# First block's steps in another order: G's two parts in unused accumulator banks, E's coefficients as a spare row of G2

## The chip, the cores and the metric

The kernel runs on one core of one Trainium2 chip. The metric is device time in microseconds; the time before is the median of five runs. A core's engines work side by side, each on a queue of its own in program order: TensorE (PE, its weight loads PEld), VectorE (DVE), ScalarE (ACT), GpSimd (POOL), and SyncE (SP), which issues most DMA transfers. An instruction that waits holds up everything behind it on its engine.

## The reference

Two layers, in float32. The first mixes each of 8 sequences with a two-dimensional Fourier transform and keeps the real part; the second is a two-layer network with a squared ReLU over all 24064 rows.

```python
# x: (8, 3008, 256)   w_in: (256, 2048)   w_out: (2048, 256)
X = np.fft.fft(np.fft.fft(x, axis=1), axis=2).real
h = X.reshape(24064, 256) @ w_in
r = np.maximum(h, 0.0)
out = (r * r) @ w_out
```

## The kernel before

The transform along the sequence becomes, for each sequence b, three arrays in SBUF: Pt (cosine part, 128 rows), Qt (sine part, 127 rows) and Et (one column of the transform, repeated on 128 partitions), each over 1505 positions. VectorE folds the input rows by symmetry (lines L356 to L386), TensorE multiplies the folded rows with cosine and sine tables (`even_n` and `odd_n`, L455 and L500, into a PSUM tile pd), and VectorE joins the partial sums (L468 to L472, tiles db, dc, then Pt, Qt, Et).

The transform along the 256 features is put into the weights instead. For each pair of 128-column chunks j of w_in (j = 0 to 7), `products` multiplies the chunk with a cosine table (cosd) and a sine table (sind, 127 columns) on TensorE into a tile pg, and ScalarE copies the two results into G1 and G2 (L263). The coefficient gE of Et is a third product, of the chunk with a column of alternating signs (altd): eight matmuls of one column (L268), halved by ScalarE into gE (L270).

The weights arrive as 64-bit floats. `convert` loads one chunk with two DMAs on SP's queue (tile raw, one of four buffers, three of which also serve the input tiles) and makes float32 of it. Its opening is two VectorE instructions (L234, L239) and three on ScalarE (L236, L237, L241); the function `finish` that it returns issues three more on VectorE (L244, L246, L247). There are 16 conversions: `load_win(j)` for w_in, tiles win, and `load_wout(j)` for w_out, tiles wout. Intermediate tile fd has two buffers, m three.

The second layer runs in steps (b, block of 251 positions, j). A step i has:
- `front`: for each of two halves h, TensorE makes hP and hQ from G1 with Pt and G2 with Qt (L551, L552), in one of two PSUM banks tagged h; VectorE adds gE times Et (L554, tile he) and forms the sum and the mirrored difference (L556, L557, tile g).
- `combine`: ScalarE applies ReLU and square (L566, L567) to g; after the first block GpSimd also forms four sums (L574 to L577).
- `back`, two steps later (LAG = 2): TensorE accumulates the product with wout in banks mA to mD. The first block uses a plain form with mA and mB alone (L591); later blocks use a form with seven products (L604).
- `gather` and `store` after the eighth j.

PSUM's eight banks are: two tagged h, two tagged d, and mA, mB, mC, mD, one each. Before the change G's products take banks of tag h, the tag of the fronts, and E's product a bank of tag d.

The order of the first eight steps is written out by hand. The conversions stand in a list, win0, win1, wout0, win2, wout1, win3 and so on, and `next_weight` opens the next one, then finishes the one opened before it, and returns its products. Ahead of the loop win0, win1 and wout0 are finished and win2 is opened. Each step of the first block then issues front, combine, back, the products of one win, and up to two calls of `next_weight`:

```python
        for f in products:
            f()
        products = [next_weight() for _ in range(2 if 0 < i < NJ - 2 else 1 if i < NJ else 0)]
```

From step 8 on, `sum_wout` (L282 to L285) and pieces of the next sequence's folding and transform are put between the fronts on VectorE (`between`); the inputs of sequence 1 are requested at step 8 (L158), followed by many small transfers of single columns (L329).

Of the kernel before, what the change touches and what calls it, by code (L numbers as in the profile page):

```python
# [13 lines left out]
P = 128  # L14
# [67 lines left out]
def kernel(  # L82
# [75 lines left out]
        nc.sync.dma_start(out=xt[b, t][0:rows], in_=x[b, r0:r0 + step * (rows - 1) + 1:step])  # L158

    cosd = const.tile([P, 2, P], F32, name="cosd")  # L160
    sind = const.tile([P, 2, P - 1], F32, name="sind")
    altd = const.tile([P, 2, 1], F32, name="altd")
    cosT = const.tile([P, 2, WT], F32, name="cosT")
    sinT = const.tile([P, 2, WT], F32, name="sinT")
    wout = const.tile([P, NJ, 2, 2, H], F32, name="wout")
    wsum = const.tile([P, 3, NJ, H], F32, name="wsum")
    ident = const.tile([P, P], F32, name="ident")
    G1 = const.tile([P, F], F32, name="G1")
    G2 = const.tile([P - 1, F], F32, name="G2")
    gE = const.tile([P, NFC], F32, name="gE")  # L170

    def load_table(tab, src, engine):
# [13 lines left out]
    ramp = const.tile([P, 2], F32, name="ramp")  # L186
    nc.vector.memset(ramp[:, 0:1], 1151.0)
    nc.vector.memset(ramp[:, 1:2], 255.0 * 2.0 ** 23)
    for dst, src in ((cosd, cos_d), (sind, sin_d), (altd, alt_d)):
        nc.scalar.dma_start(out=dst, in_=src.rearrange("(c p) m -> p c m", p=P))  # L190


# [60 lines left out]
    def load_win(j):  # L253

        w = ep.tile([P, 2, CH], F32, name="win", tag="sB" if j % 2 else "sA")
        finish = convert(parts(w, 1), pair_in(j))

        def products():
            for tab, G, n in ((cosd, G1, P), (sind, G2, P - 1)):
                ps = psh.tile([P, CH], F32, name="pg", tag="h")  # L260
                for i in range(2):
                    nc.tensor.matmul(ps[0:n], tab[:, i], w[:, i], start=i == 0, stop=i == 1)
                nc.scalar.copy(G.rearrange("p (h j f) -> j p h f", h=2, j=NJ)[j],  # L263
                               ps[0:n].rearrange("p (h f) -> p h f", h=2))
            ps = psd.tile([P, CH], F32, name="pe", tag="d")
            for h in range(2):
                for i in range(2):
                    nc.tensor.matmul(ps[:, h:h + 1], w[:, i, h * P:(h + 1) * P], altd[:, i],  # L268
                                     start=i == 0, stop=i == 1)
            nc.scalar.mul(gE[:, j::NJ], ps[:, 0:2], 0.5)  # L270

        return finish, products

    def load_wout(j):

        return convert(wout[:, j].rearrange("p h c e -> p h (c e)"), pair_out(j)), lambda: None

    def sum_wout(j):

# [261 lines left out]
    def front(b, k0, n, j, between):  # L541

        pt, qt, et = PQE[b]
        ks = slice(k0, k0 + n)
        g = gp.tile([P, 2, 2, CK], F32, name="g", tag="g")
        for h in range(2):
            fc = j + NJ * h
            fs = slice(fc * P, (fc + 1) * P)
            ps = psh.tile([P, 2, CH], F32, name="ph", tag="h")
            hP, hQ = ps[:, 0, 0:n], ps[:, 1, 0:n]  # L550
            nc.tensor.matmul(hP, G1[:, fs], pt[:, ks], start=True, stop=True)  # L551
            nc.tensor.matmul(hQ, G2[:, fs], qt[:, ks], start=True, stop=True)  # L552
            t = hp.tile([P, CK], F32, name="he", tag="he")[:, 0:n]
            nc.vector.scalar_tensor_tensor(out=t, in0=et[:, ks], scalar=gE[:, fc:fc + 1], in1=hP,  # L554
                                           op0=ALU.mult, op1=ALU.add)
            tt(out=g[:, h, 0, 0:n], in0=t, in1=hQ, op=ALU.add)  # L556
            tt(out=g[:, h, 1, 0:n][:, ::-1], in0=t, in1=hQ, op=ALU.subtract)  # L557
            between()
        return g
# [22 lines left out]
    def back(n, j, g, s, final):  # L582

        if j == 0:
            for nm in ("mA", "mB", "mC", "mD"):
                acc[nm] = psm.tile([P, 2, CH], F32, name=nm, tag=nm)
        if s is None:
            for c in range(2):
                for h in range(2):
                    for side, nm in enumerate(("mA", "mB")):  # L590
                        nc.tensor.matmul(acc[nm][:, h, 0:n], wout[:, j, h, c], g[:, c, side, 0:n],  # L591
                                         start=j == c == h == 0, stop=j == NJ - 1 and c == 1, skip_group_check=True)
            return
        products = [("mA", 0, wout[:, j, 0, 0], g[:, 0, 0]),
                    ("mA", 1, wout[:, j, 0, 1], g[:, 1, 0]),
                    ("mB", 0, wsum[:, 2, j], g[:, 1, 1]),
                    ("mB", 1, wout[:, j, 1, 0], s[:, 0]),
                    ("mC", 0, wsum[:, 0, j], s[:, 1]),
                    ("mC", 1, wsum[:, 1, j], s[:, 2]),
                    ("mD", 0, wout[:, j, 1, 1], s[:, 3])]  # L600
        if final and j == NJ - 1:
            products = products[0:2] + products[4:7] + products[2:4]
        for nm, i, w, v in products:
            nc.tensor.matmul(acc[nm][:, i, 0:n], w, v[:, 0:n], start=j == 0 and i == 0, stop=j == NJ - 1,  # L604
                             skip_group_check=True)

    def gather(n, plain, final):


        mA, mB, mC, mD = (acc[nm] for nm in ("mA", "mB", "mC", "mD"))  # L610
        if plain:
            c = ep.tile([P, 2, 2, CK], F32, name="c", tag="c")
            for side, m in enumerate((mA, mB)):
                nc.scalar.copy(c[:, side, :, 0:n], m[:, :, 0:n])
            return c
        sA = ep.tile([P, 2, CK], F32, name="sA", tag="sA")
        sB = ep.tile([P, 2, CK], F32, name="sB", tag="sB")
        u = ep.tile([P, 3, CK], F32, name="u", tag="u")
        c = ep.tile([P, 2, 2, CK], F32, name="c", tag="c")
        nc.scalar.copy(sA[:, :, 0:n], mA[:, :, 0:n])  # L620
        if not final:
            nc.scalar.copy(sB[:, :, 0:n], mB[:, :, 0:n])
        m1, m2, m4, m5 = sA[:, 0, 0:n], sA[:, 1, 0:n], sB[:, 0, 0:n], sB[:, 1, 0:n]
        u2, u3, u4 = (u[:, i, 0:n] for i in range(3))
        tt(out=u2, in0=m1, in1=mC[:, 0, 0:n], op=ALU.add)
        tt(out=u3, in0=u2, in1=mC[:, 1, 0:n], op=ALU.add)
        tt(out=u4, in0=u2, in1=mD[:, 0, 0:n], op=ALU.add)
        gt = nc.gpsimd.tensor_tensor
        gt(out=c[:, 0, 0, 0:n], in0=m1, in1=m2, op=ALU.add)
        if final:  # L630
            tt(out=c[:, 0, 1, 0:n], in0=u4, in1=mB[:, 1, 0:n], op=ALU.add)
            tt(out=c[:, 1, 1, 0:n], in0=u3, in1=mB[:, 1, 0:n], op=ALU.add)
            tt(out=c[:, 1, 0, 0:n], in0=u3, in1=mB[:, 0, 0:n], op=ALU.subtract)
            return c
        gt(out=c[:, 1, 0, 0:n], in0=u3, in1=m4, op=ALU.subtract)
        gt(out=c[:, 1, 1, 0:n], in0=u3, in1=m5, op=ALU.add)
        gt(out=c[:, 0, 1, 0:n], in0=u4, in1=m5, op=ALU.add)
        return c
# [41 lines left out]
                + groups + [(0.0, lambda: load_e(1))])  # L680


    weights = [lambda j=j: load_win(j) for j in range(2)]
    for j in range(NJ):
        weights.append(lambda j=j: load_wout(j))
        if j + 2 < NJ:
            weights.append(lambda j=j: load_win(j + 2))

    def next_weight():

        nonlocal begun
        (finish, products), begun = begun, weights.pop(0)() if weights else None
        finish()
        return products

    pieces = [fold(0, t) for t in range(NT)]
    start, *groups = [f for _, f in dft_ops(0)]

# [8 lines left out]
    def groups_at(*which):  # L707
        for i in which:
            groups[i]()

    begun = weights.pop(0)()
    for t in range(NT):
        load_x(0, t)
    load_table(cosT, cos_s, nc.sync)
    load_table(sinT, sin_s, nc.sync)
    start()
    for_p(0)
    finish, products = begun
    finish()
    products()  # L720
    for t in range(1, 4):
# [3 lines left out]
    for_q(0)  # L725
    for_q(1)
    groups_at(1, 2)
    for_p(5)
    groups_at(6, 7)
    for_p(6)  # L730
# [4 lines left out]
    groups_at(9, 10)  # L735
    for_q(6)
    groups_at(11, 12, 13)
    begun = weights.pop(0)()
    groups_at(15)
    for_q(2)  # L740
    groups_at(14, 16, 17, 18)
    for_q(3)
    groups_at(20, 19, 25)
    products = [next_weight()]
    groups_at(21, 22, 23, 26, 27, 28)
    next_weight()
    groups_at(24, 29)
    LAG = 2
    BLOCKS = [(k0, min(CK, NKT - k0)) for k0 in range(0, NKT, CK)]
    steps = [(b, k0, n, j) for b in range(B) for k0, n in BLOCKS for j in range(NJ)]  # L750
# [3 lines left out]
    def between():  # L754


        nonlocal spent
        if i < NJ or i % NJ == LAG - 1:
            return
        spent -= pace / 2 if i < 2 * NJ else pace  # L760
        while side and spent <= 0:
            t, f = side.pop(0)
            f()
            spent += t

    flight, finished = [], []
    for i in range(len(steps) + LAG + 4):
        if i < len(steps):
# [12 lines left out]
                spent, pace = 0.0, sum(t for t, _ in side) / (calls - (0 if i else 3 * (NJ - 1)))  # L781
            g = front(b, k0, n, j, between)
            if i < NJ:
                s = combine(n, g, True)
            elif i < 2 * NJ:
                sum_wout(j)
        while finished and finished[0][0] <= i:
            store(*finished.pop(0)[1:])
        if i >= LAG and flight:
# [3 lines left out]
            if at[3] == NJ - 1:  # L793
                c_ = gather(at[2], s_ is None, final)
                finished += [(i + 2 + s, *at[:3], s, c_, final) for s in range(2)]
        for f in products:
            f()
        products = [next_weight() for _ in range(2 if 0 < i < NJ - 2 else 1 if i < NJ else 0)]
        if i < len(steps):
            flight.append(((b, k0, n, j), g, s if i < NJ else combine(n, g, False)))  # L800

# [62 lines left out]
```

## Time and profile before

| What | Value |
|---|---|
| Time, median of 5 runs (range) | 1962.86 us (1962.1 to 1964.76) |
| The profiled execution: time, span | 1963.19 us, 1961.4 us |
| Mean granted TensorE clock | 0.996 |
| Busy in the span: PE, DVE, ACT, POOL | 1924.5, 1399.3, 924.9, 1170.3 us |
| First he (L554) of steps 0, 1, 2, 3 | 53.59, 59.69, 68.19, 76.69 us |
| First he of steps 6, 7, 8, 9, 10 | 102.19, 108.28, 113.32, 118.43, 123.53 us |

Times inside a trace count from the span's first instruction. The profiled execution's own time is 1.8 us longer than its span. A line of a timeline gives start, duration, engine, source line, operation and tiles; what stands in brackets is the idle time just before and who ended it. Instructions of one engine overlap at their ends, so the room that one takes is read from start to start.

### The profile page before, as it was taken

What the parts mean: (1) busy time and instruction counts of PE and PEld (TensorE: products, weight loads), DVE (VectorE), ACT (ScalarE), POOL (GpSimd) and SP (SyncE); (2) the same over time, 40 slices, a digit from 0 to 9 for tenths busy, and PEclk for the clock granted to TensorE, in tenths of its full rate; (3) what the DMA queues carried; (4) which work ended last, traced back from release to release, by engine and by line L of the source; (5) the groups of instructions that cost most, each with busy time, mean ns of one, the idle gap of its engine ahead of it and who ended that gap; (6) DMA issues with size and microseconds to landing.
All of it is one profiled execution on the core that took longest, in us unless ns stands there. A gap on an engine that the chain in (4) does not pass through costs nothing.

```text
span 1961.4 us, 27513 instructions
## 1 busy us (share of the span) xinstructions
PE 1924.5 (98%) x9160; PEld 1705.1 (87%) x9160; DVE 1399.3 (71%) x3434; ACT 924.9 (47%) x1076; POOL 1170.3 (60%) x1705
## 2 busy tenths in 40 slices
PE   5999999999999999999999999999999999999998
PEld 3788888888988899888998889888898888988887
DVE  7888867777677776777668776677767777655554
ACT  1754544455444444444444454444544454444443
POOL 0036745667466755666556765666756676556564
PEclk8999999999999999999999999999999999999999
DMA  7332101211021111111011200121002101100101
GB/s 194 111 45 53 26 13 40 49 27 23 13 51 41 23 26 27 41 33 35 12 35 36 46 20 12 37 52 27 20 16 52 33 11 22 27 11 11 22 11 22
DMA packets 145340, 68.88 MB, mean 35 GB/s; under 512 B 129003, under 2 KB 136110, under 8 KB 145197
## 3 DMA queue, kind: packets, MB, share of 16 engines
q1 hardware_dynamic: 144121, 66.60, 15.6%
q8 instruction: 72, 1.18, 0.3%
q14 instruction: 71, 0.58, 0.1%
q10 hardware_dynamic: 1076, 0.52, 0.1%
HBM read 42.39 MB, written 24.68 MB: 34 GB/s over the span
## 4 chain that ended last, share of the span: by engine, by line
PE 92%; DVE 4%; ACT 1%; DMA 1%; issue 0%; POOL 0%; SPq 0%; DVEq 0%; POOLq 0%; ACTq 0%
PE ph L552 16%; PE ph L551 16%; PE mC L604 16%; PE mA L604 16%; PE mB L604 16%; PE mD L604 8%; PE pd L455 2%; PE pd L500 2%; DVE he L554 1%; DVE g L557 1%; DVE g L556 1%; DMA cosT<-in_cos_s_dram 0%; ACT g L566 0%; ACT g L567 0%; DVE w L386 0%
## 5 line engine op out<-in xcount | busy, mean ns | idle before, releaser
L566 ACT ACTIVATE g<-g 128x1004 f32<-128x1004 f32 (+1 forms) x384 | 399.5, 1040 | 817.7 <-DVE g L557 383.0
L574 POOL TENSOR_TENSOR s<-g 128x251 f32<-128x251 f32 (+1 forms) x376 | 246.0, 654 | 716.2 <-ACT g L567 654.5
L554 DVE SCALAR_TENSOR_TENSOR he<-Et,gE,ph 128x251 f32<-128x251 f32 (+1 forms) x768 | 361.6, 471 | 422.0 <-PE ph L552 421.0
L551 PE MATMUL ph<-Pt,G 128*128 128x251 f32 (+1 forms) x1536 | 451.8, 375 | 4.6 <-ACT G L263 3.4
L552 PE MATMUL ph<-Qt,G 127*128 127x251 f32 (+1 forms) x1536 | 451.4, 374 | 0.4 <-DVE Qt L468 0.4
L567 ACT ACTIVATE g<-g 128x1004 f32<-128x1004 f32 (+1 forms) x384 | 399.3, 1040 | 12.2
L604 PE MATMUL mC<-s,wsum 128*128 128x251 f32 (+1 forms) x1504 | 381.4, 374 | 0.0
L604 PE MATMUL mA<-g,wout 128*128 128x251 f32 (+1 forms) x1504 | 379.8, 374 | 0.0
L556 DVE TENSOR_TENSOR g<-he,ph 128x251 f32<-128x251 f32 (+1 forms) x768 | 320.4, 417 | 54.4 <-POOL s L574 0.5
L551 PEld LDWEIGHTS ph<-Pt,G 128*128 128x128 f32 x1536 | 287.3, 189 | 42.7 <-ACT G L263 4.0
L552 PEld LDWEIGHTS ph<-Qt,G 127*128 127x128 f32 x1536 | 291.2, 190 | 36.6 <-DVE Qt L468 0.8
L604 PEld LDWEIGHTS mC<-s,wsum 128*128 128x128 f32 x1504 | 285.6, 190 | 34.6
L557 DVE TENSOR_TENSOR g<-he,ph 128x251 f32<-128x251 f32 (+1 forms) x768 | 314.1, 409 | 0.0
L604 PEld LDWEIGHTS mA<-g,wout 128*128 128x128 f32 x1504 | 282.8, 189 | 34.8 <-issue 0.6
L575 POOL TENSOR_TENSOR s<-s,g 128x251 f32<-128x251 f32 (+1 forms) x376 | 283.4, 754 | 29.4
L576 POOL TENSOR_TENSOR s<-g 128x251 f32<-128x251 f32 (+1 forms) x376 | 295.4, 786 | 0.0
L577 POOL TENSOR_TENSOR s<-g,s 128x251 f32<-128x251 f32 (+1 forms) x376 | 255.4, 679 | 0.0
L604 PE MATMUL mB<-g,wsum 128*128 128x251 f32 (+1 forms) x752 | 220.5, 374 | 0.0
L604 PE MATMUL mD<-s,wout 128*128 128x251 f32 (+1 forms) x752 | 220.4, 374 | 0.0
L604 PE MATMUL mB<-s,wout 128*128 128x251 f32 (+1 forms) x752 | 219.9, 374 | 0.0
L604 PEld LDWEIGHTS mB<-g,wsum 128*128 128x128 f32 x752 | 142.6, 190 | 17.4
L604 PEld LDWEIGHTS mD<-s,wout 128*128 128x128 f32 x752 | 141.9, 189 | 17.7
(118 smaller groups left out, 1284.0 us busy)
## 6 DMA issues: line engine op xcount, KB each, us to landing
out_dram<-os SPq DMA_DIRECT2D x376, 56.0 KB
xt<-in_x_dram SPq DMA_DIRECT2D x32, 384.0 KB
xt<-in_x_dram SPq DMA_DIRECT2D x42, 128.0 KB
Et<-e_dram SPq DMA_DIRECT2D x7, 752.5 KB
xt<-in_x_dram SPq DMA_DIRECT2D x9, 512.0 KB
out_dram<-os SPq DMA_DIRECT2D x288, 6.8 KB
raw<-in_moe_w_in_dram SPq DMA_DIRECT2D x16, 256.0 KB
raw<-in_moe_w_out_dram SPq DMA_DIRECT2D x16, 256.0 KB
```

The lines of the kernel that those rows point to most:

```text
L551: nc.tensor.matmul(hP, G1[:, fs], pt[:, ks], start=True, stop=True)
L552: nc.tensor.matmul(hQ, G2[:, fs], qt[:, ks], start=True, stop=True)
L554: nc.vector.scalar_tensor_tensor(out=t, in0=et[:, ks], scalar=gE[:, fc:fc + 1], in1=hP, op0=ALU.mult, op1=ALU.add)
L556: tt(out=g[:, h, 0, 0:n], in0=t, in1=hQ, op=ALU.add)
L557: tt(out=g[:, h, 1, 0:n][:, ::-1], in0=t, in1=hQ, op=ALU.subtract)
L566: act(v, v, AF.Relu)
L567: act(v, v, AF.Square)
L574: gt(out=s1, in0=g21, in1=g22, op=ALU.add)
L575: gt(out=s2, in0=s1, in1=g11, op=ALU.subtract)
L576: gt(out=s3, in0=g11, in1=g21, op=ALU.subtract)
L577: gt(out=s4, in0=g12, in1=s2, op=ALU.subtract)
L604: nc.tensor.matmul(acc[nm][:, i, 0:n], w, v[:, 0:n], start=j == 0 and i == 0, stop=j == NJ - 1, skip_group_check=True)
```

## The change

1. The first block's steps get another order. Each step issues front, then (in `weights`) the opening of a wout, the products of win i+1, the finish of win i+2 and the opening of win i+3; then combine and back; then (in `rest`) E's product, the finish of the wout and gE's scaling. wout0 is no longer converted ahead of the loop; wout5 and wout6 are both opened and finished in step 6, wout7 in step 7.
2. G's two products go to the banks mC and mD, which the plain `back` no longer allocates.
3. The alternating column becomes the 128th column of sind, so that G2 has 128 rows, the last of which holds E's coefficients. `for_e` brings that row onto partitions with two products against the last column of the identity (in place of four against altd), and VectorE, in place of ScalarE, halves it into gE. The fronts read the first 127 rows of G2. For win0, `for_e` and its scaling are issued after `groups_at(1, 2)` instead of right after the products.

```diff
-    sind = const.tile([P, 2, P - 1], F32, name="sind")
-    altd = const.tile([P, 2, 1], F32, name="altd")
+    sind = const.tile([P, 2, P], F32, name="sind")
...
-    G2 = const.tile([P - 1, F], F32, name="G2")
+    G2 = const.tile([P, F], F32, name="G2")
...
-    for dst, src in ((cosd, cos_d), (sind, sin_d), (altd, alt_d)):
+    for dst, src in ((cosd, cos_d), (sind[:, :, 0:P - 1], sin_d), (sind[:, :, P - 1:], alt_d)):
...
         def products():
-            for tab, G, n in ((cosd, G1, P), (sind, G2, P - 1)):
-                ps = psh.tile([P, CH], F32, name="pg", tag="h")
+            for tab, G, nm in ((cosd, G1, "mC"), (sind, G2, "mD")):
+                pg = psm.tile([P, CH], F32, name="pg", tag=nm)
                 for i in range(2):
-                    nc.tensor.matmul(ps[0:n], tab[:, i], w[:, i], start=i == 0, stop=i == 1)
+                    nc.tensor.matmul(pg, tab[:, i], w[:, i], start=i == 0, stop=i == 1)
...
+        def for_e():
+
             ps = psd.tile([P, CH], F32, name="pe", tag="d")
             for h in range(2):
-                for i in range(2):
-                    nc.tensor.matmul(ps[:, h:h + 1], w[:, i, h * P:(h + 1) * P], altd[:, i],
-                                     start=i == 0, stop=i == 1)
-            nc.scalar.mul(gE[:, j::NJ], ps[:, 0:2], 0.5)
-
-        return finish, products
+                fc = j + NJ * h
+                nc.tensor.matmul(ps[:, h:h + 1], G2[:, fc * P:(fc + 1) * P], ident[:, P - 1:], start=True, stop=True)
+
+            return lambda: nc.vector.tensor_scalar_mul(gE[:, j::NJ], ps[:, 0:2], 0.5)
+
+        return finish, products, for_e
...
-            nc.tensor.matmul(hQ, G2[:, fs], qt[:, ks], start=True, stop=True)
+            nc.tensor.matmul(hQ, G2[0:P - 1, fs], qt[:, ks], start=True, stop=True)
...
-            for nm in ("mA", "mB", "mC", "mD"):
+            for nm in ("mA", "mB") if s is None else ("mA", "mB", "mC", "mD"):
...
     groups_at(1, 2)
+    for_e()()
     for_p(5)
...
-    begun = weights.pop(0)()
+    win.append(load_win(1))
     groups_at(15)
     for_q(2)
     groups_at(14, 16, 17, 18)
     for_q(3)
     groups_at(20, 19, 25)
-    products = [next_weight()]
-    groups_at(21, 22, 23, 26, 27, 28)
-    next_weight()
-    groups_at(24, 29)
+    win.append(load_win(2))
+    win[1][0]()
+    groups_at(21, 22, 23, 26, 27, 28, 24, 29)
...
+    def weights():
+
+
+        now = i - 1 if i < NJ - 1 else i
+        late = [load_wout(now)] if now >= 0 else []
+        if i + 1 < NJ:
+            win[i + 1][1]()
+        if i + 2 < NJ:
+            win[i + 2][0]()
+        if i + 3 < NJ:
+            win.append(load_win(i + 3))
+        elif i == NJ - 2:
+            late.append(load_wout(i))
+
+        def rest():
+            if i + 1 < NJ:
+                late.append(win[i + 1][2]())
+            for f in late:
+                f()
+
+        return rest
...
             g = front(b, k0, n, j, between)
             if i < NJ:
+                rest = weights()
                 s = combine(n, g, True)
...
-        for f in products:
-            f()
-        products = [next_weight() for _ in range(2 if 0 < i < NJ - 2 else 1 if i < NJ else 0)]
+        if i < NJ:
+            rest()
```

More of the change, by code (lines that the diff above doesn't have):

```diff
@@ L258, in products @@
         def products():
-            for tab, G, n in ((cosd, G1, P), (sind, G2, P - 1)):
-                ps = psh.tile([P, CH], F32, name="pg", tag="h")
+            for tab, G, nm in ((cosd, G1, "mC"), (sind, G2, "mD")):
+                pg = psm.tile([P, CH], F32, name="pg", tag=nm)
                 for i in range(2):
-                    nc.tensor.matmul(ps[0:n], tab[:, i], w[:, i], start=i == 0, stop=i == 1)
+                    nc.tensor.matmul(pg, tab[:, i], w[:, i], start=i == 0, stop=i == 1)
                 nc.scalar.copy(G.rearrange("p (h j f) -> j p h f", h=2, j=NJ)[j],
-                               ps[0:n].rearrange("p (h f) -> p h f", h=2))
+                               pg.rearrange("p (h f) -> p h f", h=2))
+        def for_e():
             ps = psd.tile([P, CH], F32, name="pe", tag="d")
             for h in range(2):
-                for i in range(2):
-                    nc.tensor.matmul(ps[:, h:h + 1], w[:, i, h * P:(h + 1) * P], altd[:, i],
-                                     start=i == 0, stop=i == 1)
-            nc.scalar.mul(gE[:, j::NJ], ps[:, 0:2], 0.5)
-        return finish, products
+                fc = j + NJ * h
+                nc.tensor.matmul(ps[:, h:h + 1], G2[:, fc * P:(fc + 1) * P], ident[:, P - 1:], start=True, stop=True)
+            return lambda: nc.vector.tensor_scalar_mul(gE[:, j::NJ], ps[:, 0:2], 0.5)
+        return finish, products, for_e
     def load_wout(j):
-        return convert(wout[:, j].rearrange("p h c e -> p h (c e)"), pair_out(j)), lambda: None
+        return convert(wout[:, j].rearrange("p h c e -> p h (c e)"), pair_out(j))
     def sum_wout(j):
@@ L607, in gather @@
     def gather(n, plain, final):
-        mA, mB, mC, mD = (acc[nm] for nm in ("mA", "mB", "mC", "mD"))
+        mA, mB = acc["mA"], acc["mB"]
         if plain:
@@ L615, in gather @@
             return c
+        mC, mD = acc["mC"], acc["mD"]
         sA = ep.tile([P, 2, CK], F32, name="sA", tag="sA")
@@ L680, in ahead @@
                 + groups + [(0.0, lambda: load_e(1))])
[L683 to L694, printed above, removed]
     pieces = [fold(0, t) for t in range(NT)]
@@ L709, in groups_at @@
             groups[i]()
-    begun = weights.pop(0)()
+    win = [load_win(0)]
     for t in range(NT):
@@ L717 @@
     for_p(0)
-    finish, products = begun
+    finish, products, for_e = win[0]
     finish()
@@ L737 @@
     groups_at(11, 12, 13)
-    begun = weights.pop(0)()
+    win.append(load_win(1))
     groups_at(15)
```

## The prediction

> **What bounds the kernel now.** I read the page's busy times and slices first: TensorE is busy for 98% of the span, and only the first slices fall short.
>
> ```profile
> PE 1924.5 (98%) x9160; PEld 1705.1 (87%) x9160; DVE 1399.3 (71%) x3434; ACT 924.9 (47%) x1076; POOL 1170.3 (60%) x1705
> ...
> PE   5999999999999999999999999999999999999998
> ```
>
> The change touches only the stretch ahead of the first block and that block's eight steps, so I cut the trace into those steps with the view of windows (a step begins at the first he L554 of its front):
>
> ```profile
> 76.69:85.19 8.50, 8.01 (x42) 6.94 (x41) 7.58 (x17) 6.50 (x12) 0.00 (x0) 1.00 0.37 124
> 108.28:123.53 15.25, 15.25 (x73) 13.56 (x72) 12.63 (x31) 7.00 (x15) 2.61 (x4) 1.00 0.34 69
> 123.53:157.36 33.83, 33.07 (x154) 28.51 (x152) 32.19 (x81) 14.25 (x14) 20.43 (x28) 1.00 0.44 34
> 36.50:39.20 2.70, 0.00 (x0) 0.00 (x0) 2.63 (x8) 2.12 (x4) 0.00 (x0) 1.00 1.02 357
> 39.30:42.60 3.30, 3.00 (x5) 1.84 (x6) 2.69 (x9) 0.00 (x0) 0.00 (x0) 0.50 0.03 9
> ```
>
> Columns: stretch, length, then busy time of TensorE, its weight loads, VectorE, ScalarE, GpSimd, then the granted clock. In a middle step (8.50 us) TensorE works 8.01 and VectorE 7.58: two engines nearly full, each waiting a little for the other through ScalarE. From 123.53 to 157.36 VectorE is the full one. So the account is kept on VectorE, up to the front of step 10 at 123.53. Its waits in 50 to 125 us, then one step of it by the timeline:
>
> ```profile
> DVE he L554 <- PE ph L552: 4.7, 6, 1.2
> DVE fd L244 <- ACT fd L237: 3.8, 5, 0.8
> ```
>
> ```profile
> 68.19 0.47 DVE L554 SCALAR_TENSOR_TENSOR he<-Et,gE,ph 128x251 f32<-128x251 f32 x1
> ...
> 70.52 0.42 DVE L234 TENSOR_SCALAR fd<-raw 128x512 uint32<-128x512 uint32 x1
> ...
> 71.19 0.68 DVE L244 SCALAR_TENSOR_TENSOR fd<-raw,fd 128x512 uint32<-128x512 uint32 x1
> ...
> 73.24 0.43 DVE L234 TENSOR_SCALAR fd<-raw 128x512 uint32<-128x512 uint32 x1
> ...
> 74.76 0.69 DVE L244 SCALAR_TENSOR_TENSOR fd<-raw,fd 128x512 uint32<-128x512 uint32 x1 [0.76 <-ACT fd L237]
> ...
> 76.69 0.47 DVE L554 SCALAR_TENSOR_TENSOR he<-Et,gE,ph 128x251 f32<-128x251 f32 x1
> ```
>
> By starts: front 2.33; a conversion's opening pair 0.67; its finish 2.05 or 1.93. So 2.33 + 0.67 + 2.05 + 0.67 + 1.93 = 7.65 of work, and 0.85 in which the second finish waits for ScalarE, which runs relu, square, the G copies and gE before it comes to that conversion. This wait recurs in five steps. Before, the steps 0 to 9 take 6.10, five times 8.50, 6.09, 5.04, 5.11 and 5.10: 69.94 us in all.
>
> **The change, part by part.**
>
> *The steps in the new order.* The finish in mid-step now belongs to a conversion opened a step earlier, so ScalarE is done with it. The wout finish comes last; its ScalarE part stands first in ScalarE's queue and is done 2.5 after its L234 starts, while VectorE comes to it only after 0.67 + 1.93 + 0.67 = 3.3. TensorE's next front no longer shares its banks with G's products, so it runs ahead of VectorE: the 4.7 us of he waits go, but for the first 0.33. VectorE's step becomes its own work:
> - step 0: 2.33 + 1.93 + 0.67 + gE 0.18 = 5.1
> - steps 1 to 4: 7.65 + gE 0.18 + about 0.04 for a buffer change = 7.87 each, 31.5
> - step 5 (one opening pair fewer): 7.1
> - step 6 opens and finishes wout5 and wout6 in one step. L237 ends 1.95 after its L234 starts (0.46 + 1.49), VectorE has 1.34 of opening pairs: 0.64 of waiting; the second finds the G copies (0.52) and two ScalarE conversions ahead: 0.53. 7.65 + 0.18 + 1.17 = 9.0
> - step 7 opens wout7 and finishes it at once: 2.33 + 0.67 + 1.31 waiting + 1.95 = 6.26
> - steps 8 and 9, now never waiting: 4.84 and 3.65 (5.11 and 5.10 less their start-to-start waits).
> Sum 67.5 against 69.94: **2.45 us gained**. What is late next is VectorE itself: it does not wait between 123.53 and 161 in the trace, so the shift passes through; from there TensorE is full (busy 1779.57 of the 1780 us from 170 to 1950) and carries it to the end. E's product takes four matmuls for eight, 0.45 for the row's 0.95; a step then costs TensorE some 7.5, under VectorE's 7.87, so this part earns nothing itself.
>
> *gE on VectorE.* ScalarE's 128x2 op (median 187 ns, next start 0.07 later) goes; VectorE gets seven in the loop. No row is that narrow: below stands a 128x1 memset at 0.059, above a 128x94 add from PSUM at 0.246. I take 0.18 (the 94 columns start 0.16 apart, and the next he must wait for gE's end): 1.26 in the sums above, 0.4 to 1.7 at the ends. Behind it in VectorE's queue stands the next front; it waits for two E products that TensorE reaches only after back(i-2). By the rows (products 1.73, back 3.41, E 0.45) they are done about 1.4 before gE's turn in steps 2 to 5.
>
> *Ahead of the block.* The conversion of wout0 (0.67 + 1.93) leaves, but the last Qt joins then wait for TensorE's twelve matmuls from 47.97 to 52.01: only 0.2 is gained. Against it, win0's gE now stands in VectorE's queue right after join_2 (ends 23.23): its products need that bank, queue behind the second even_n (ScalarE's copy of that starts at 24.00), and take 0.45 to 0.9. VectorE stalls 1.4 to 1.8, all folds behind it. The cover is the 1.35 wait at 36.30 for win1's raw landing, which does not move; 0.05 to 0.45 remains, I take 0.2, and without the cover it would be 1.6. Net of both: 0. The loads keep their order on SP's queue and landed 3.3 us after issue in the steps, against a step of lead. x(1,0) to x(1,2) now wait for wout5, 6 and 7 instead of win7, wout6, wout7: due at VectorE 9 us later, against 3.5 to land. cosd, sind, alternating column: the same three transfers.
>
> *A new gap on TensorE, in step 1.* No back exists yet there. E's product for step 2 waits for the G2 copy, and ScalarE has before it win3's three ops (from 58.3), relu and square of step 0, wout0's three, and the copies: 58.3 + 2.0 + 2.1 + 2.0 + 0.6 = 65.0. TensorE's last work ends at 60.1: 4.9 us idle. What idling does is in two rows:
>
> ```profile
> 32.45 2.17 PE L455 MATMUL pd<-cosT,w 128*128 128x377 f32 x6 [1.14 <-DVE Pt L472]
> ...
> 39.60 3.65 PE L455 MATMUL pd<-cosT,w 128*128 128x376 f32 x6 [3.19 <-DVE Et L472]
> ```
>
> After 3.19 idle the clock was 0.50 (window above) and six like matmuls took 3.65 instead of 2.17; after 2.27 idle, at 47.97, it was 1.00. At half clock, E and the first half-front take 2.6 instead of 1.3, and VectorE's front of step 2 comes 1.2 late; 0.8 if the clock opens soon, 1.9 if it stays half for 6.8 us as at 18.75; nothing if it falls and rises within the gap. I take 1.1.
>
> [...]
>
> Sum: 2.45 - 1.1 = 1.35. The profiled execution before took 1963.19 (span 1961.4 and 1.8 around it), 0.33 above the median of 1962.86; so about 1961.8 in its terms and **1961.4** as a median.
>
> **The rivals.**
> *Everything falls well (0.20).* No clock loss, gE at 0.06 (0.84 saved), the prelude's stall wholly covered (0.2), and the half clock at 39.3 not repeated because TensorE's work now lies later in the stretch before it (up to 0.9): 2.45 + 0.84 + 0.2 + 0.9 = 4.4, 1958.5. For it: each is seen in a row. Against: all are needed.
> *gE becomes the wait that replaces the old one (0.15).* If TensorE is 1.4 later than I lay it out, VectorE waits for E in each of four steps, some 0.5 each: 2 us back, with the clock's 1.1 about 1963.4, no change. For it: a product between two copies on three engines. Against: the 1.4.
> *The clock stays half (0.10), the case on the slower side.* In step 1, after the 4.9 gap, TensorE at half clock needs some 15 us for a step of 7.87. Count in stretches as long as the half-clock one at 39.3, some 3.4 us: two cost 1.9, three about 3.5, and from there it decides, for that eats the gain; five cost some 7.5, and the time is 1962.9 - 2.45 + 7.5 = 1968. For it: at 18.75 it stayed half for 6.8 us under steady small matmuls. Against: at 39.3 it recovered in 3.4 us under wide ones, which these are.
> That the change does nothing to VectorE's waits would contradict the new order of queues; it is within the second rival.
>
> **How the numbers follow.** Forecast 0.55, rivals 0.20, 0.15, 0.10. A measurement of this kernel tells apart about 0.2%, 3.9 us. Only the first rival passes that downward (0.20), only the third upward (0.10), the rest is within (0.70). The range runs from 1958.0, the first rival less half a microsecond of the runs' own spread (their lowest is 0.76 under the median), to 1964.4, which takes in the second rival and the forecast with its worst terms (gE 0.25, clock 1.9, stall uncovered: 1961.4 + 0.5 + 0.8 + 1.4) and as much spread; the third is left out.
>
> **What would show it.** Right: L244's waits gone except in steps 6 and 7, VectorE steps of 7.9, gE rows of 0.15 to 0.25, a TensorE gap of 5 us near 60 to 65 and a clock of 0.50 behind it, step 10's front near 122, everything past 160 shifted alike. Wrong: he waiting for gE's products in every step, raw landings as releasers, or a steady stage whose length differs.

## The result, and the profile after

| | Kernel before | Changed kernel |
|---|---|---|
| Time, median (range; runs) | 1963.76 us (1960.01 to 1966.95; 50) | 1965.93 us (1962.76 to 1969.43; 30) |
| Ratio to before, 95% interval | | 1.0011 [1.0006, 1.0016] |
| Profiled execution: time, span, clock | 1963.19, 1961.4, 0.996 | 1966.84, 1965.0, 0.992 |
| First he of steps 0, 1, 2, 3 | 53.59, 59.69, 68.19, 76.69 | 55.81, 60.99, 70.00, 79.15 |
| First he of steps 8, 9, 10, 11 | 113.32, 118.43, 123.53, 128.97 | 117.70, 122.40, 126.45, 132.58 |
| Last he | 1941.90 | 1945.55 |

The change costs about 2.2 us where the prediction had a gain of 1.4, and the time lies above the predicted range. In the two profiles everything after step 11 is shifted alike, by 3.6 to 3.7 us, so the whole difference of these two executions is made ahead of 132.58: 0.65 of it ahead of the first fold on VectorE (8.42 for 7.77), while x lands, the rest in the stretch that the prediction looked at. The medians put the difference at 2.2.

Lines of the changed kernel in the code have moved: he is now L556, E's product L270, its scaling on VectorE L272, the G copies L262, a conversion's finish L243, `even_n` and `odd_n` L457 and L502. The first view is the page of the changed kernel: busy times, and the slices of TensorE and of its granted clock.

```profile
PE 1926.8 (98%) x9128; PEld 1705.5 (87%) x9128; DVE 1403.1 (71%) x3442; ACT 924.5 (47%) x1068; POOL 1170.6 (60%) x1705
...
PE   5899999999999999999999999999999999999998
...
PEclk8899999999999999999999999999999999999999
```

There are 32 fewer matmuls (E's product), and yet TensorE is busy 2.3 us longer: its instructions got longer, not more. The second slice is 8 where it was 9 before. Next the view of windows, cut at the steps' first he and at the stretches of half clock; columns as in the prediction.

```profile
60.99:70.00 9.01, 4.90 (x19) 3.99 (x18) 7.64 (x18) 8.85 (x15) 0.00 (x0) 0.82 0.40 132
70.00:79.15 9.15, 9.15 (x37) 7.82 (x37) 7.76 (x18) 6.57 (x11) 0.00 (x0) 0.80 0.32 102
87.44:95.36 7.92, 7.43 (x38) 6.31 (x37) 7.64 (x17) 6.15 (x11) 0.00 (x0) 1.00 0.36 128
126.45:161.42 34.97, 33.33 (x155) 28.71 (x154) 33.34 (x82) 14.36 (x15) 20.53 (x28) 1.00 0.43 32
46.33:53.16 6.83, 5.45 (x9) 3.14 (x10) 3.19 (x11) 1.32 (x3) 0.00 (x0) 0.50 0.25 79
39.50:46.30 6.80, 4.60 (x22) 3.26 (x22) 6.66 (x18) 1.47 (x5) 0.00 (x0) 1.00 0.15 58
66.81:73.64 6.83, 6.58 (x18) 5.48 (x19) 5.11 (x13) 4.43 (x7) 0.00 (x0) 0.50 0.46 150
19.03:32.68 13.65, 12.23 (x29) 8.02 (x30) 10.73 (x32) 0.48 (x2) 0.00 (x0) 0.50 0.77 202
```

Step 4 (87.44) is the step that was predicted: 7.92, with VectorE at 7.64. Steps 1 and 2 are not: 9.01 and 9.15, and in step 2 TensorE is busy for all of it at a mean clock of 0.80. Before, the clock was 0.50 from 18.75 to 25.57 and from 39.23 to 42.64; now it is so for 13.65, 6.83 and 6.83 us. (The clock record of a trace begins some way into the span, here at 15.34 and 15.61; the view counts what lies ahead of it as 1.00, but the matmuls there run at half rate: in the changed kernel four of 256 columns take 2.08 us at 12.15 and 1.03 at 56.46.) The waits of VectorE from 50 to 135 us, and below them TensorE's timeline at the two later places:

```profile
DVE Qt L470 <- PE pd L457: 4.9, 2, 3.3
DVE he L556 <- PE ph L554: 3.2, 5, 1.2
DVE fd L243 <- ACT fd L236: 2.2, 3, 1.2
```

```profile
40.63 2.17 PE L457 MATMUL pd<-cosT,w 128*128 128x376 f32 x6 [1.74 <-DVE Et L474]
...
47.71 6.73 PE L457 MATMUL pd<-sinT,w 128*127 128x377 f32 x12 [2.28 <-ACT raw L240]
```

```profile
67.06 1.01 PE L270 MATMUL pe<-ident,G 128*128 128x1 f32 x4 [4.11 <-ACT G L262]
67.94 1.19 PE L553 MATMUL ph<-Pt,G 128*128 128x251 f32 x2
68.92 1.04 PE L554 MATMUL ph<-Qt,G 127*128 127x251 f32 x2
```

The wait for ScalarE's conversions fell from 3.8 to 2.2, as the new order meant it to. In its place VectorE waits for TensorE: 4.9 us for the Q parts, whose twelve matmuls take 6.73 where they took 4.04, and 3.2 us for fronts, the longest of which run at half rate behind a gap of 4.11 (a pair of 251 columns takes 1.04 to 1.19 there, 0.59 to 0.67 at 78.01 with a clock of 1.00). The six matmuls for Et at 40.63, in turn, took 2.17 instead of 3.65: the half clock did not only grow, it moved.

### The profile page after: what moved, and what is told of

It is laid out like the page before. It is cut to its first block, busy times and chain, and to the rows that moved or that the text cites. A ratio compares the mean times of both kernels' runs of the same rounds, so it can differ in the third digit from the quotient of the medians.

```text
span 1965.0 us, 27465 instructions
## 1 busy us (share of the span) xinstructions
PE 1926.8 (98%) x9128; PEld 1705.5 (87%) x9128; DVE 1403.1 (71%) x3442; ACT 924.5 (47%) x1068; POOL 1170.6 (60%) x1705
## 4 chain that ended last, share of the span: by engine, by line
PE 93%; DVE 4%; DMA 1%; ACT 1%; issue 1%; POOL 0%; SPq 0%; DVEq 0%; ACTq 0%; POOLq 0%
PE ph L554 16%; PE ph L553 16%; PE mC L606 16%; PE mA L606 16%; PE mB L606 16%; PE mD L606 8%; PE pd L457 3%; PE pd L502 2%; DVE he L556 1%; DVE g L558 1%; DVE g L559 1%; DMA cosT<-in_cos_s_dram 0%; DMA xt<-in_x_dram 0%; DVE w L388 0%; PE pg L261 0%
## 5 line engine op out<-in xcount | busy, mean ns | idle before, releaser
L556 DVE SCALAR_TENSOR_TENSOR he<-Et,gE,ph 128x251 f32<-128x251 f32 (+1 forms) x768 | 361.7, 471 | 418.7 <-PE ph L554 417.0
L577 POOL TENSOR_TENSOR s<-s,g 128x251 f32<-128x251 f32 (+1 forms) x376 | 282.9, 752 | 29.5
```

The source lines that it names most:

```text
L577: gt(out=s2, in0=s1, in1=g11, op=ALU.subtract)
```

## The experiments

**The clock theory**: the reorder opens gaps on TensorE, and the half clock behind them costs more than VectorE's ledger gains. **The order theory**, its rival: the new order, the banks or the spare row cost the time by themselves, and the clock is a side effect. They are told apart by giving TensorE something to do in its idle places. `fill` issues matmuls of 128x256 from the cosine table into the bank mA, which nothing else uses at that time.

```python
    def fill(count):
        ps = psm.tile([P, CH], F32, name="fill", tag="mA")
        for _ in range(count):
            nc.tensor.matmul(ps, cosd[:, 0], cosd.rearrange("p c m -> p (c m)"), start=True, stop=True)
```

In the tables, "ahead" is the time from the profile's first fold on VectorE to the first he, and "block" from there to the first he of step 11. A profile shows a single execution, and the executions of one kernel differ (the mean granted clock of the changed kernel's thirty is 0.990 to 0.996; of what some expectations call the clock's phase the runs show no more); so the medians and their intervals decide, and the profiles tell where.

The column on half clock goes by the clock record of each trace, and "to 34.20" says where that record begins, no more. Ahead of it the view of windows gives 1.00, for it has nothing to count, but in the traces of before, after and e3 the first matmuls run at half rate. In e3, whose record begins at 34.20, the same four matmuls of 256 columns:

```profile
12.51 2.08 PE L261 MATMUL pg<-win,cosd 128*128 128x256 f32 x4 [12.51 <-DMA xt<-in_x_dram]
...
54.50 1.03 PE L261 MATMUL pg<-win,cosd 128*128 128x256 f32 x4
```

In the same trace matmuls of 376 or 377 columns start 0.63 us apart up to 33.9 and 0.32 apart from 36.1 on. In the kernel before the same four take 2.07 us at 11.50, and 1.02 at 78.27. So these three don't start at full rate, and the records begin at different times, from 15.34 in the kernel before to 34.20 in e3.

### TensorE's idle places filled

**e1_fill_step1.** The changed kernel, with the matmuls in step 1 alone.

```diff
+        if i == 1:
+            fill(9)
```

> Theory 1 (clock): the change's gain on VectorE is there (2.45 us), but TensorE drops to half clock after the 4.1 us gap in step 1 and again under Q's matmuls ahead of the block. Nine idle-time matmuls in step 1 (3.9 us of work that nothing reads) hold the clock at 1.00: steps 1, 2 and 3 take 7.9 us each instead of 9.01, 9.15 and 8.29, up to 2.8 less than the changed kernel; as the phase of the clock differs between executions, 1 to 2.5 less in the median, 1963.5 to 1965 for the 1965.9. Theory 2 (queue order): the time is lost because VectorE waits for E's product behind back and the copies whatever the clock; the extra matmuls stand ahead of that product and make it later: 1966 or more, step 1 to 3 as long as before.

**e2_fill_ahead.** The changed kernel, with eight ahead of the block.

```diff
     groups_at(15)
+    fill(3)
...
     groups_at(20, 19, 25)
+    fill(5)
```

> Three and five extra matmuls (nothing reads them) in TensorE's two gaps ahead of the first block. Theory 1: the twelve matmuls of Q take 4.0 us instead of 6.7, the first he comes at 53.5 instead of 55.8; as the phase differs between executions, 0.5 to 2 less than the changed kernel in the median, 1964 to 1965.4. Theory 2: not less than the changed kernel, 1966 to 1967.

**e3_fill_both.** Both of these.

> Both fillings. Theory 1: the losses are separate and add: the first he near 53.5, every step of the first block at its own work, span about 1960 to 1961.5 in the profiled execution and a median of 1961 to 1963, below the kernel before (ratio 0.998 to 0.9995). Theory 2: 1966 or more.

**e4_before_fill.** The kernel before, with six and five such matmuls at the same two places ahead of the block.

> The kernel before with six and five such matmuls in its own gaps ahead of the block, as a control. Theory 1: its one half-clock stretch there (39.2 to 42.6, 1.5 us of loss on six matmuls, 1.2 us on VectorE) goes, up to 1.2 us less, ratio 0.9994 to 1.0000. So the changed kernel loses because it has more half-clock time, not because any clock loss is new. Theory 2: no change, or slower by what is added.

| Kernel | Median, us | Ratio to before [95%] | Half clock ahead of 135 us | Ahead | Block |
|---|---|---|---|---|---|
| before | 1963.61 | 1 | to 15.34, 18.75–25.57, 39.23–42.64 | 45.82 | 75.38 |
| after | 1965.93 | 1.0011 [1.0006, 1.0016] | to 15.61, 19.03–32.68, 46.33–53.16, 66.81–73.64 | 47.39 | 76.77 |
| e1 | 1964.0 | 1.0002 [0.9993, 1.0011] | to 33.80 | 46.32 | 74.52 |
| e2 | 1963.38 | 0.9998 [0.9989, 1.0007] | to 15.73, 19.14–32.80, 63.52–70.34 | 44.73 | 76.82 |
| e3 | 1961.84 | 0.9992 [0.9984, 1.0001] | to 34.20 | 45.08 | 74.50 |
| e4 | 1961.6 | 0.9991 [0.9982, 1.0000] | to 24.43 | 44.20 | 75.36 |

(After's median is from its own runs; its ratio compares it with the kernel before beside it.) The view of windows of e3, in its steps 1 and 2:

```profile
59.04:66.98 7.94, 7.69 (x39) 6.51 (x38) 7.65 (x18) 7.81 (x14) 0.00 (x0) 1.00 0.38 124
66.98:74.91 7.93, 7.93 (x41) 7.02 (x40) 7.65 (x17) 6.93 (x12) 0.00 (x0) 1.00 0.44 134
```

The clock is 1.00 for 0.82 and 0.80, and steps 1 and 2 take 7.94 and 7.93 for 9.01 and 9.15: VectorE's work, 7.65 in each, now fills its step. Work was added and the kernel became faster: e3 against after is 1.0011 - 0.9992 = 0.0019, some 3.7 us. Of that the filling in step 1 alone gives 0.0009 (1.8 us) and the one ahead 0.0013 (2.6 us); each of these differences is uncertain by about 0.0010, so the two can't be told apart, while their joint effect is clear. The kernel before gains 0.0009 (1.8 us, with an interval that just reaches zero), more than the 1.2 expected at most: it had paid for a half clock of its own. With both filled, the two kernels can't be told apart, 1961.84 and 1961.6, and the loss of 2.2 is gone. So the clock accounts for the sign. But the change was to gain 2.45 in its block, and there, with a recorded clock of 1.00 in both, e3 is only 0.86 shorter than e4 (74.50 for 75.36).

### Parts of the change alone

**p2_banks_only.** The kernel before, with G's products in mC and mD and nothing else.

```diff
-            for tab, G, n in ((cosd, G1, P), (sind, G2, P - 1)):
-                ps = psh.tile([P, CH], F32, name="pg", tag="h")
+            for tab, G, n, nm in ((cosd, G1, P, "mC"), (sind, G2, P - 1, "mD")):
+                ps = psm.tile([P, CH], F32, name="pg", tag=nm)
...
-            for nm in ("mA", "mB", "mC", "mD"):
+            for nm in ("mA", "mB") if s is None else ("mA", "mB", "mC", "mD"):
```

> The kernel before with G's products in mC and mD and nothing else. If the spare row is what made the kernel with both parts in the old order 8 us slower (E's product, behind the G2 copy, stands between that copy and the next front on TensorE: 9.29 us a step instead of 8.50): steps of 8.50, ratio 0.9995 to 1.0005. If the banks did it: ratio about 1.003.

Measured: 1964.7 us against 1964.86 beside it, ratio 1.0002 [0.9993, 1.0011], the block 75.37 with the same steps of 8.50. The banks alone change nothing that these runs can show.

**p1_old_order.** The kernel before, with the banks and the spare row, in the old order; ScalarE still scales gE.

> The kernel before with the two other parts of the change alone: G's products in mC and mD, E's coefficients as the 128th row of G2 (four one-column matmuls for eight), gE still scaled by ScalarE, the steps in the old order. Theory 1 (all that moves the time comes from the new order, by VectorE's waits and TensorE's clock): the five waits of 0.76 us at L244 stay, steps of 8.50 us stay, ratio to before 0.9995 to 1.0005. Theory 3 (the banks or the spare row cost the time themselves, since E's product now waits for the copy of G2): slower, ratio about 1.001 as in the changed kernel.

Measured: 1971.82 us, ratio 1.0036 [1.0023, 1.0048], the block 82.91, some of it at half rate (a pair of matmuls of 251 columns takes 1.04 us at 70.77 and 0.59 at 73.80). This expectation failed. The waits of VectorE and of TensorE from 54 to 135 us, and TensorE's timeline in step 1:

```profile
DVE fd L243 <- ACT fd L236: 9.8, 5, 2.9
DVE he L552 <- PE ph L550: 6.1, 6, 1.8
```

```profile
PE pe L267 <- ACT G L262: 11.5, 7, 2.7
```

```profile
60.42 0.61 PE L267 MATMUL pe<-ident,G 128*128 128x1 f32 x4 [2.61 <-ACT G L262]
...
60.89 0.67 PE L549 MATMUL ph<-Pt,G 128*128 128x251 f32 x2
```

With altd, E's product needed only win and followed G's products at once. From the spare row it needs ScalarE's copy of G2, which stands behind relu and square, and the next front stands behind it on TensorE: seven waits, 11.5 us. So parts 1 and 3 of the change belong together; the new order puts E's product after back, and in after the same wait is 5.5 us, 4.1 of it in step 1 where there is no back yet.

### The places named by the profile, mended

**e5_gE_early.** After, with win0's E product right after its products and the scaling after the third fold.

```diff
     products()
+    half = for_e()
...
+    half()
...
-    for_e()()
```

> The changed kernel with win0's E product right behind its G products and its scaling on VectorE after the third fold, so that VectorE doesn't stand 1.4 us behind join_2. If the raw landing covers most of that stall, as I forecast: the wait at L233 for the landing comes back by 0.6 to 1.0 us, the first he comes 0.4 to 0.8 earlier at equal clock, and the median falls by no more than 0.8 against the changed kernel (1965.1 to 1966). If the stall is what costs: 1.4 or more less (1964.5 or below).

Measured: 1965.12 us, ratio 1.0009 [1.0000, 1.0018]. Against after (1.0011) that tells nothing; its profile had half clock in step 1 again (62.70 to 69.52). In it the stall at gE is gone and a wait of 1.0 us for the raw landing is back, as was expected.

**e6_copies_first.** After, with the products of win i+1 issued ahead of the opening of the wout, so that the G copies come three ScalarE instructions earlier.

```diff
-        late = [load_wout(now)] if now >= 0 else []
         if i + 1 < NJ:
             win[i + 1][1]()
+        late = [load_wout(now)] if now >= 0 else []
```

> The changed kernel with the products of win i+1 issued ahead of the opening of wout, so that the G copies stand ahead of three ScalarE instructions. No work is added. Theory 1 (clock): TensorE's gap in step 1 falls from 4.1 to about 2.3 us, the clock stays 1.00 in steps 2 and 3 in more executions, 0.5 to 2 less than the changed kernel (1964 to 1965.4). Theory 2 (queue order apart from the clock): only the later opening of wout counts, L243 of wout waits 0.1 to 0.5 in four steps, 1966 to 1967.5.

Measured: 1963.22 us, ratio 0.9997 [0.9989, 1.0006]. TensorE's gap in step 1 is 2.2 for 4.1, steps 1 and 2 take 7.92 and 7.95, though 3.41 us of step 1 and 2 (68.34 to 71.75) were at half clock, and step 6 takes 8.44 for 8.97. Its profile still had the Q parts at half clock. The median fell by more than either theory said.

**e7_wout0_ahead.** After, with wout0 converted ahead of the loop again and each wout a step earlier.

> The changed kernel with wout0 converted ahead of the loop as in the kernel before, and each wout one step earlier. Ahead of the block VectorE idles 2.2 us (at full clock) to 4.9 us for Q's matmuls, so the 2.6 us of conversion cost at most 0.5 there. In the loop VectorE's steps 0 to 7 fall from 59.6 (at full clock) to about 55.3; TensorE then needs about as much (8 steps of 7.4), so 1 to 4 less than the changed kernel, 1962 to 1965, with the clock loss of step 1 still in it. Were VectorE not the longer engine of the block (theory 2), nothing would be gained: 1966.

Measured: 1964.5 us, ratio 1.0004 [0.9995, 1.0013], and steps 0 to 7 take 59.1 us, well above what was expected: VectorE waited 5.4 for fronts and TensorE 7.0 for G copies, since more of ScalarE's conversions now stand ahead of them (e10 moves the copies forward). Steps 8 to 10 take 5.11, 5.11 and 5.48.

**e12_first_early.** e5 and e6 together, nothing filled.

> The changed kernel with the G copies ahead of wout's opening and win0's gE early; no work is added. The two edits gave 2.7 and 0.8 us by themselves; theory 1 has them independent (one acts in step 1, the other ahead of the block): 1962.0 to 1963, ratio 0.9990 to 0.9997. Were both only one thing (the clock's phase): 1963.2 as with the copies alone.

**e8_early_first_fill.** e12 with both fillings.

> The same with the idle-time matmuls in both places. The clock is then full throughout, so what is left is the change's own balance: step 10's 0.7 us of contention with GpSimd stays, the stall ahead of the block is gone. 1960.5 to 1961.8, no more than 1 us below the kernel before with filling (1961.6). Theory 2, that the order itself is slower than the old one: 1962.5 or more.

**e10_wout0_first_fill.** e7, with the products ahead of the wout and both fillings.

> wout0 ahead of the loop, the G copies first, and both fillings. With wout0 ahead alone the steps 0 to 7 took 59.1 us where 55.3 was expected, because VectorE waited 5.4 us for TensorE's fronts behind E's product (7.0 us of waits for the G copies). With the copies first and the clock held, those waits should fall by half: steps 0 to 7 in 56 to 58, median 1959 to 1961, the fastest so far. If TensorE's own work bounds the block (8 steps of 7.4): 1961 to 1962.

| Kernel | Median, us | Ratio to before [95%] | Half clock ahead of 135 us | Ahead | Block |
|---|---|---|---|---|---|
| before, beside them | 1964.86 | 1 | | | |
| e12 | 1962.97 | 0.9993 [0.9984, 1.0002] | to 30.63, 40.87–44.28, 47.70–51.11, 64.76–68.18 | 46.97 | 73.98 |
| e8 | 1960.25 | 0.9979 [0.9970, 0.9988] | to 31.25 | 44.03 | 73.98 |
| e10 | 1959.44 | 0.9973 [0.9963, 0.9983] | to 15.91, 19.33–32.98 | 44.89 | 72.27 |

e12 and e8 have the same block, to the hundredth, and differ ahead by 2.94 in the profiles and by 2.7 in the medians: with the copies first the gap in step 1 costs nothing in e12's profile (its steps 1 and 2 take 7.93 each), and what is left of the clock's price lies ahead. e8 against e3 is 0.52 shorter in the block, which is step 6, and 1.05 shorter ahead; gE's stall is gone from there, but e8's recorded clock of 1.00 also begins 2.95 us earlier, so its share is not shown. e10 is the fastest of all, 5.4 us below the kernel before. Part of that is the filling: the kernel before with filling (e4) stood at 0.9991, so the order itself is worth some 2 to 3.5 us (1959.44 against 1961.6, and 0.9973 against 0.9991, taken at different times). Its steps 0 to 7 take 56.58, as expected. Its windows in step 1 and its waits of VectorE and of TensorE from 54 to 135 us:

```profile
61.04:68.96 7.92, 7.92 (x40) 6.86 (x39) 7.63 (x18) 6.55 (x11) 0.00 (x0) 1.00 0.40 132
```

```profile
DVE he L556 <- PE ph L554: 2.3, 3, 1.1
DVE fd L243 <- ACT fd L236: 1.2, 1, 1.2
```

```profile
PE pg L261 <- DVE win L246: 1.7, 4, 0.4
PE pe L270 <- ACT G L262: 0.5, 1, 0.5
```

E's product waits 0.5 us, in after 5.5; VectorE waits 3.5, in the kernel before 8.5 (4.7 and 3.8). Only the first step has become longer, 7.93 for 6.10 before, since it converts a wout.

## Why the prediction was wrong

**The block's ledger on VectorE: right in the middle, too good at its end.** With the clock at 1.00 from the first he on (e3), against the prediction's terms, from first he to first he:

| Step | Predicted | e3 | Reading |
|---|---|---|---|
| 0 | 5.1 | 5.19 | right |
| 1, 2, 4 | 7.87 each | 7.94, 7.93, 7.93 | right |
| 3 | 7.87 | 8.30 | a wait of 0.49 for the front |
| 5, 6, 7 | 7.1, 9.0, 6.26 | 7.13, 8.98, 6.23 | right, with the waits for L236 in steps 6 and 7 |
| 8 | 4.84 | 4.70 | right |
| 9 | 3.65 | 4.05 | sums of wout, stretched |
| 10 | 5.44, as before | 6.12 | sc and sums, stretched |

Step 3 contradicts "TensorE's next front no longer shares its banks with G's products, so it runs ahead of VectorE": the front stood behind E's product, which had waited 0.37 for the G2 copy, as p1 shows in the large. I had asked whether E was ready for gE, and it was; I had not asked who stands behind E. Steps 9 and 10 contradict "it does not wait between 123.53 and 161 in the trace, so the shift passes through": VectorE indeed did not wait, but its instructions grew longer. e3's timeline of VectorE in step 10, and GpSimd's in the same time:

```profile
124.56 0.98 DVE L374 TENSOR_TENSOR sc<-fs 95x258 f32<-95x258 f32 x1
125.46 0.80 DVE L284 TENSOR_TENSOR wsum<-wout 128x128 f32<-128x128 f32 x1
126.30 0.61 DVE L285 TENSOR_TENSOR wout<-wout 128x128 f32<-128x128 f32 x1
126.94 0.70 DVE L286 TENSOR_TENSOR wsum<-wout 128x128 f32<-128x128 f32 x1
127.67 0.76 DVE L287 TENSOR_TENSOR wsum<-wsum,wout 128x128 f32<-128x128 f32 x1
```

```profile
123.83 0.63 POOL L576 TENSOR_TENSOR s<-g 128x251 f32<-128x251 f32 x1 [2.31 <-ACT g L569]
124.53 0.72 POOL L577 TENSOR_TENSOR s<-s,g 128x251 f32<-128x251 f32 x1
125.21 0.91 POOL L578 TENSOR_TENSOR s<-g 128x251 f32<-128x251 f32 x1
126.08 0.67 POOL L579 TENSOR_TENSOR s<-g,s 128x251 f32<-128x251 f32 x1
```

A sum takes 0.28 to 0.29 us while GpSimd idles and 0.61 to 0.80 here; sc takes 0.98, where in the kernel before it took 0.45. Since fronts no longer hold VectorE back in steps 8 to 10 (in the kernel before by 0.69, 0.32 and 1.16), these instructions meet GpSimd's first sums (four in each step) at another moment. In e10, where the front of step 10 waits 1.09 for TensorE again, sc takes 0.42 and the step 5.48. In e3 sc starts 0.03 after GpSimd's L577 and ends 0.29 after it; why an instruction beside GpSimd's takes longer was not shown.

Together: 0.43 in step 3, 0.40 and 0.68 in steps 9 and 10, 0.1 in all the others. Of the 2.45, 0.86 is left (75.36 of e4 less 74.50 of e3).

**Ahead of the block: the stall came, and what it costs is not settled.** The prediction took 0.2 of gE's stall as uncovered and 0.2 as gained. The stall is there as laid out, and so is the row's price:

```profile
25.25 0.16 DVE L272 TENSOR_SCALAR gE<-pe 128x2 f32<-128x2 f32 x1 [1.42 <-PE pe L270]
```

The cover that was named, the 1.35 wait for a raw landing, is gone from the waits of after, and where gE is moved out of the way it comes back: 1.0 us in e5's profile, 1.4 in e12's, 0.4 in e8's. The gain at the end is there too: from the first of Q's matmuls (43.36 in e3, 41.16 in e4) to the first he, e3 takes 10.49 and e4 10.70. Yet the whole stretch ahead is 0.88 longer in e3 than in e4 (45.08 for 44.20). That can't be put down to the stall, for the recorded clock of 1.00 begins at 34.20 in e3 and at 24.43 in e4, and at 34.59 VectorE waits 0.95 for TensorE in e3 and not in e4. No run here has the two orders ahead of the block at the same clock.

**The clock: the effect was named, its place and size were not.** The gap in step 1 was predicted at 4.9 us near 60 to 65 and was 4.11, ending at 67.06, with a clock of 0.50 behind it. I took 1.1 of loss, with 1.9 as its upper end; e1 makes it 1.8, and in after's profiled execution, where the half clock lasted 6.83, steps 1 and 2 are 9.01 - 7.94 and 9.15 - 7.93 longer than in e3, 2.3 together. The larger failure is that the prediction priced the clock in step 1 only. The twelve Q matmuls at 47.97 stood in the trace of before with a granted clock of 1.00 and a gap of 2.27 ahead, and that was taken as safe; in after the same gap, 2.28, has them at half clock, 2.7 us longer. e2 puts the price of the clock ahead of the block at 2.6 us in after, and e4 at 1.8 in the kernel before: 0.8 more, where the forecast had no change and the first rival a gain of 0.9. Both prices are uncertain by nearly 2 us; the 2.7 on the Q matmuls is measured, in one execution.

In all, against the 1.35 of the sum: the block 1.6 less, the clock 0.7 more in step 1 and 0.8 more ahead. That is 3.1, and makes about 1.8 of loss where 2.2 [1.2, 3.1] was measured; this needs no further loss by gE's stall, and does not exclude one. So the steps of the prediction that failed are the clock, priced at 1.1 in one place and at nothing ahead of the block, and the 2.45 of the block, of which 0.86 came. The rest of the distance from 1961.4 is the median of before, 1962.86 in five runs and 1963.76 in fifty.

**The rivals.** None came as written. The third had the sign and the mechanism (half clock in step 1), but its price was for five stretches there; the profile has 6.83 us, two of them, which by the rival's own 1.9 would still have left a gain. The slower side was reached by the sum of several terms that the prediction had small or at nothing. The second (gE's product as the new wait) is in step 3 with 0.49, not in four steps. The first did not come: the clock was lost in two places, and gE took 0.16. e10, which comes near its 1958.5, is another order, with a busy TensorE. Of the signs of being right most came (L243 waits in steps 6 and 7 alone, steps of 7.9, a gE row of 0.16, the gap and the half clock behind it); step 10's front came at 126.45 instead of near 122.

**What lay ahead of the falls.** The shortest half clock in the traces of before and after lasted 3.41 us (39.23 to 42.64), and TensorE's busy time in as long a stretch ahead of each fall differs. Ahead of the fall at 66.81 it has no matmul at all, in the gap of 4.11. Ahead of the fall at 46.33 it was busy for 2.31 (for 4.60 in the last 6.80 us), in matmuls of 94 to 376 columns, and the longest wait near by was 2.28, which began only 0.9 ahead of the fall. In the kernel before it was busy for 0.81 and 0.60 ahead of the falls at 18.75 and 39.23, in the changed kernel for 0.22 ahead of that at 19.03. So the clock fell here behind an idle stretch, and behind stretches in which TensorE was partly busy.

**What stays open.** What exactly makes the clock fall ahead of the block (the share of busy time, the narrow matmuls, or something else) was not settled. Busy time alone does not tell: 2.31 of the last 3.41 us were busy ahead of the fall at 46.33, and in the kernel before only 1.50 of 46.06 to 49.47, where the clock stayed at 1.00. Without filling ahead of the block, after's profile has the Q parts at half clock and e1's at 1.00, and each shows one execution. The filling comes too late for the half clock up to about 33 us, which e2, e3 and e10 all have; what that part costs, and with it the stall at gE, stays open.

## What to carry to other kernels

Here a reorder that freed VectorE left TensorE idle for 4.11 us, and the half clock, 6.83 us of it behind that gap and 6.83 under the Q matmuls, cost more than the reorder gained: filling gave back some 3.7 us here and 1.8 in the kernel before, and the block's gain was 0.86. So list TensorE's gaps of the new order, all the way up to the place of the change, and for every instruction that is made to wait ask who stands behind it on its queue. Give way first to what TensorE waits for (here the G copies ahead of a conversion: 4.1 us of gap became 2.2 and lost its price), and where a gap can't be closed, a few matmuls that nothing reads can be worth more than they cost (17 of them gave those 3.7 us). To tell a clock loss from a loss of order, fill the gaps in both kernels and compare again, and check a clock of 1.00 in a view against the durations of equal matmuls (2.08 and 1.03 us in e3).

## What the runs showed of the hardware that was not expected

- Matmuls that nothing reads made the changed kernel faster by 0.0019 of its time and e12 by 0.0014; the kernel before by 0.0009, with an interval that just reaches zero.
- In the profiles of before, after and e3 TensorE's first matmuls run at half rate (in e3 four of 256 columns take 2.08 us at 12.51 and 1.03 at 54.50), though the view of windows gives a clock of 1.00 there; in e3 those of 376 or 377 columns start 0.63 us apart up to 33.9 and 0.32 from 36.1 on.
- In before and after the recorded half clock ahead of 135 us lasted 3.4, 6.8 or 13.7 us, and it came also after a stretch that was not idle: 4.60 of 6.80 us busy ahead of 46.33. From 19.03 to 32.68 it stayed half with TensorE busy 12.23 of 13.65 us.
- An add of 128x128 on VectorE took 0.29 us alone and 0.80 or 0.81 beside GpSimd's sums, in both kernels; step 10 came earlier in e3 and took 6.12 us for 5.44.
